# The late groups of a feed-forward network on seven products of halves: 256 tokens and a quarter of d_ff at a step, in place of 384 tokens and an eighth

## The chip, the cores and the metric

The kernel runs on one core of a Trainium2 chip. The metric is the device time of one execution in microseconds. The engines are named as in the profile: PE is TensorE (products), PEld its weight loads, DVE VectorE, ACT ScalarE, POOL GpSimd, SP the engine that issues most of the transfers.

## What is computed

Eight batches of eight heads, 576 tokens, head size 64, with 32 memory slots per head; then a feed-forward network on 4608 tokens (512 to 2048 to 512).

```python
a = exp(phi - max_over_tokens(phi)); a = a / (sum(a) + 1e-09)      # phi: 8,8,576,32
k_m = einsum('bhsm,bhsd->bhmd', a, k)
v_m = einsum('bhsm,bhsd->bhmd', a, v)
scores = q @ k_m^T / sqrt(64)
attn = softmax(scores)                                             # over 32 slots
x = (attn @ v_m)  as 4608 x 512
h = x @ w_in                                                       # 512 x 2048
out = maximum(0.01 * h, h) @ w_out                                 # 2048 x 512, all in float32
```

## The kernel before

v_m and w_in are multiplied first, batch by batch: the folded matrix W (256 rows of heads and slots by 2048) takes the place of v_m and w_in, so that a token needs attn @ W. That is the fold: `fold(b, j)` makes quarter j of W of batch b, with 24 small products on parts of the array (L722). A product of two float32 matrices is three products of 16-bit halves: high by high, low by high, high by low. A high half is made by ScalarE (a CAST or a scaled copy), the low one by DVE (value less high half). Of W, ScalarE makes the high half (L745) and DVE the low one (L746).

The feed-forward network runs over 12 groups G of 384 tokens (three for two batches) and 8 units u of 256 columns of d_ff each. `up_products` (L806) multiplies the tokens' attention weights a by W into a bank of PSUM, two banks a unit (f16: 6 products of 384 columns for each half of a unit, or 12 of 192 in the groups that lie across two batches). `activate` applies the leaky rectifier with ScalarE (Prelu, L813), makes the high half g with DVE (L821) and the low half (L822). `down` (L861) multiplies g by w_out into three banks, 18 products of 512 columns a unit, and keeps on adding to them over all units of the group; `store` (L840) scales and sends 128 rows.

All five engines run in the order in which the code issues: there is no scheduler. `OPENING` is a list of steps written by hand: group G0, in float32, with the loading of the weights, batches 0 and 1, and products of ones (`z`, L928) that fill gaps. Then comes `slot(n)` for each unit n from 5 on: ups of unit n+3, fold, attention steps of the list `before`, `activate`, the splits of the fold, attention steps of `after`, down of unit n, attention steps of `ends`. The lists say at which slot which step of the attention of a later batch runs: A1 to C4 make the softmax of phi, C10 the product with k and v (L485), D and Q transposes (L600 for Q), E10 to E22 the scores (L621), S01 the maximum over memory slots (L655, DVE), S02 its subtraction (L658, GpSimd), S03 the exponential (L663, ScalarE), S04 to S08 the normalisation and the halves of a (L685, L689, L693). The table `SPLIT` spreads the making of the halves of w_in and w_out (`k`: L279 ScalarE, `l`: L284 DVE) over slots 6 to 22.

## Time and profile before

| what | value |
|---|---|
| median of 3 runs | 689.25 us (688.81 to 689.81) |
| profiled execution | 688.93 us, of it 687.2 us span |
| granted TensorE clock, mean | 0.992 |
| busy: PE, PEld | 673.7 us, 371.1 us |
| busy: DVE, ACT, POOL | 390.9 us, 269.8 us, 52.9 us |
| instructions | 14105 |

The span goes from the first to the last instruction; what the runs' time has above it lies around it. Busy times are shares of the span per engine. Matmuls of one stream overlap in the records, so the distance between two starts, and not the duration of one, says what a product costs in a stream.

### The profile page before, as it was taken

The page shows a single profiled execution, that of the slowest core. Times are in us where ns is not written, and L with a number is a line of the kernel's source. Part 1 is how long each engine was busy: PE and PEld are TensorE (multiplying, and loading weights), DVE is VectorE, ACT ScalarE, POOL GpSimd, SP SyncE. Part 2 cuts the span into 40 slices and gives each one's busy share as a digit, 9 for nine tenths or more (in the row PEclk, how much of TensorE's full clock was granted, in tenths as well). Part 3 has the DMA queues.
Part 4 walks back from the last instruction along what each step waited for, and adds up shares of the span by engine and source line. Part 5 has one row for each costly group of instructions (what it writes and reads, how often), then busy time and mean ns, then how long its engine had stood idle before and what let it go on. Part 6 is the DMA issues. An engine that isn't in the chain of part 4 may idle for free.

```text
span 687.2 us, 14105 instructions
## 1 busy us (share of the span) xinstructions
PE 673.7 (98%) x6142; PEld 371.1 (54%) x6142; DVE 390.9 (57%) x586; ACT 269.8 (39%) x441; POOL 52.9 (8%) x42
## 2 busy tenths in 40 slices
PE   7899999999999999999999999999999999999997
PEld 6545446665454546665545445565545545655553
DVE  5775876966887563445685473544584654332220
ACT  2699666643444323312332432421332342322321
POOL 0000130000210120000120120000120030000000
PEclk9799999999999999999999999999999999999999
DMA  9999504613503400204503500303500100100101
GB/s 267 401 317 281 201 1 143 179 47 109 135 16 125 115 1 1 82 2 138 150 1 124 128 5 1 82 1 105 139 12 2 48 1 1 47 2 0 47 1 46
DMA packets 32590, 60.16 MB, mean 88 GB/s; under 512 B 4368, under 2 KB 14608, under 8 KB 32528
## 3 DMA queue, kind: packets, MB, share of 16 engines
q1 hardware_dynamic: 32240, 58.87, 28.5%
q8 instruction: 48, 0.79, 0.5%
q10 hardware_dynamic: 288, 0.39, 0.2%
q14 instruction: 14, 0.11, 0.1%
HBM read 49.81 MB, written 9.44 MB: 86 GB/s over the span
## 4 chain that ended last, share of the span: by engine, by line
PE 94%; DVE 2%; issue 1%; ACT 1%; DMA 1%; ACTq 0%; DVEq 0%
PE po L861 55%; PE ph L806 29%; PE pa L722 4%; PE pa L621 2%; PE pa L485 2%; DMA out_dram<-ob 1%; PE pa L550 1%; PE pa L436 0%; DMA wi<-in_phi_dram 0%; DVE W L746 0%; DVE r1k L406 0%; PE pa L211 0%; ACT wi L274 0%; PE pa L499 0%; ACT ob L840 0%
## 5 line engine op out<-in xcount | busy, mean ns | idle before, releaser
L861 PE MATMUL po<-wo,g 128*128 128x512 f16 (+1 forms) x1680 | 399.5, 392 | 0.0
L861 PEld LDWEIGHTS <-g 128*128 128x128 f16 x1584 | 152.7, 98 | 183.1 <-issue 11.0
L806 PE MATMUL ph<-a,W 128*128 128x192 f16 (+2 forms) x1504 | 210.9, 293 | 0.1
L813 ACT ACTIVATE gf<-ph,g_sc 128x384 f32<-128x384 f32 x176 | 99.4, 580 | 220.0 <-PE ph L806 175.3
L821 DVE CAST g<-gf 128x768 f16<-128x768 f32 x88 | 61.6, 700 | 190.7 <-ACT gf L813 190.6
L806 PEld LDWEIGHTS <-W 128*128 128x128 f16 x1440 | 129.2, 98 | 55.0 <-issue 5.1
L822 DVE TENSOR_TENSOR g<-gf,g 128x768 f16<-128x768 f32 x88 | 84.3, 958 | 3.0
L658 POOL TENSOR_TENSOR t<-t,tm 128x1152 f32<-128x1152 f32 (+2 forms) x9 | 15.9, 1770 | 429.7 <-DVE tm L655 429.7
L722 PE MATMUL pa<-wi,vT 64*32 64x512 f16 (+1 forms) x704 | 29.9, 420 | 2.4 <-issue 2.0
L746 DVE SCALAR_TENSOR_TENSOR W<-pa,W 128x512 f16<-128x512 f32 x48 | 30.7, 681 | 0.0
L861 PEld LDWEIGHTS po<-wo,g 128*128 128x128 f32 x96 | 17.6, 190 | 21.0 <-issue 19.4
L840 ACT ACTIVATE ob<-po,osc 128x512 f32<-128x512 f32 x28 | 18.8, 688 | 25.1 <-PE po L861 23.2
L745 ACT ACTIVATE W<-pa 128x512 f16<-128x512 f32 x48 | 26.1, 599 | 2.4 <-PE pa L722 1.9
L600 DVE STREAM_TRANSPOSE ld<-ld 96x1536 f32<-96x1536 f32 x14 | 24.0, 1750 | 2.2 <-PE pa L485 2.2
L663 ACT ACTIVATE t<-t 128x1152 f32<-128x1152 f32 (+2 forms) x10 | 9.7, 972 | 33.8 <-POOL t L658 31.4
L260 ACT ACTIVATE ld<-ld 128x768 f32<-128x768 f32 (+1 forms) x24 | 19.9, 840 | 4.3 <-DMA ld<-in_moe_w_in_dram 4.2
L693 POOL TENSOR_TENSOR a<-t,a 128x1152 f16<-128x1152 f32 (+2 forms) x9 | 18.5, 2053 | 40.0 <-ACT a L689 35.8
L635 DVE STREAM_TRANSPOSE t<-pa 128x384 f32<-128x384 f32 x24 | 12.3, 557 | 15.1 <-PE pa L621 15.1
L520 ACT ACTIVATE x_k<-pa,r 128x192 f32<-128x192 f32 x14 | 5.1, 417 | 39.7 <-PE ph L806 38.1
L689 ACT CAST a<-t 128x1152 f16<-128x1152 f32 (+2 forms) x9 | 8.7, 970 | 26.9 <-DVE t L685 26.9
L806 PEld LDWEIGHTS ph<-a,W 128*128 128x128 f32 x64 | 12.1, 199 | 9.6 <-issue 3.5
L485 PE MATMUL pa<-ld 64*32 64x128 f32 x1008 | 16.1, 271 | 0.5 <-issue 0.5
(157 smaller groups left out, 428.6 us busy)
## 6 DMA issues: line engine op xcount, KB each, us to landing
ld<-in_q_dram SPq DMA_DIRECT2D x16, 576.0 KB, 6.6
out_dram<-ob SPq DMA_DIRECT2D x138, 64.0 KB, 1.7
ld<-in_k_dram SPq DMA_DIRECT2D x28, 288.0 KB, 5.0
ld<-in_v_dram SPq DMA_DIRECT2D x28, 288.0 KB, 5.6
ld<-in_moe_w_in_dram SPq DMA_DIRECT2D x12, 512.0 KB, 7.3
ld<-in_moe_w_out_dram SPq DMA_DIRECT2D x12, 512.0 KB, 7.6
ld<-in_phi_dram SPq DMA_DIRECT2D x7, 576.0 KB, 7.5
ld<-in_moe_w_in_dram SPq DMA_DIRECT2D x8, 256.0 KB, 8.2
```

The costliest lines, as they stand in the source:

```text
L260: nc.scalar.activation(hi.bitcast(F32), hi.bitcast(F32), AF.Prelu, scale=2.0**-111, alpha=-(2.0**32))
L485: nc.tensor.matmul(var["pk"][g][hh * M:(hh + 1) * M, cs], ld["phi"][rows, hh, j, :], ld["kv", hh][rows, kinds[0]:kinds[-1] + 1, j, :], sta ...
L600: nc.vector.transpose(flat, ld["q", g].rearrange("p hh j d -> p (hh j d)"))
L722: nc.tensor.matmul(pf[g][cols, :], lhs, rhs, start=(n == 0), stop=(n == len(passes) - 1), tile_position=(g * D, hh * M),)
L745: nc.scalar.activation(w[:, g, 0], src[g], AF.Copy, scale=ws)
L746: nc.vector.scalar_tensor_tensor(w[:, g, 1], src[g], ws, w[:, g, 0], ALU.mult, ALU.subtract)
L806: nc.tensor.matmul(ph[:, t0:t0 + n * SB], lhs, rhs, start=(m == 0), stop=(m == len(seq) - 1))
L813: nc.scalar.activation(dst, ph, AF.Prelu, scale=sc, alpha=SLOPE)
L821: nc.vector.tensor_copy(g[:, 0], gf)
L822: nc.vector.tensor_tensor(g[:, 1], gf, g[:, 0], ALU.subtract)
L840: nc.scalar.activation(ob, po, AF.Copy, scale=so)
L861: nc.tensor.matmul(po, lhs, rhs, start=(f == 0 and m == 0), stop=(f == NQ * NF - 1 and m == len(seq) - 1),)
```

## The change

G0 to G2 (the first two batches) stay as they were. From token 1152 on there are 13 groups of 256 tokens and one of 128, with four steps each: a step k takes a quarter of d_ff (512 columns, two units). A group's output is a 2x2 matter: two halves of tokens by two halves of the 512 output columns, summed over two halves of the d_ff of the step. The eight products of such halves are replaced by seven with sums and differences of the operands (Winograd's form). For this:

- The sums of blocks of w_out are made once, in slots 5 to 15: GpSimd adds (`add_up`, L347), ScalarE makes the high half (`hi_sum`, L350), DVE the low one (`lo_sum`, L353), 16 of 128x512 of each.
- The sums of g are made in each step: `add_g` four on DVE (L1052), `hi_g` two CASTs on ScalarE (L1056), `lo_g` two differences on DVE (L1060).
- `up_late` (L1017) makes four blocks a step, each 6 products of 256 columns (or two by six, where the group lies across two batches), in turn in the two halves of one bank; the Prelu (L1029) frees a half.
- `down_late` (L1084) takes 42 products of 256 columns a step, in four parts of 12, 12, 6 and 12, into four banks: `p1` and three of the group. After a group's fourth step `combine` adds them up (L1094 to L1103) and scales (L1106).
- The order of a step: up(0), part(0), up(1), part(1), `ends`, up(2), part(2), up(3), fold of step k+3 (L817, splits L841 and L842), part(3), `ends`. The ups are those of step k+2.
- Attention steps are placed by a table, batch to first slot and spread. The loads of Q move from the end of the batch before to behind C10 (here L562); S07 and S08 (L779, L784) write a in another layout, in three pieces; L735 is S01, L743 is S03, L680 the transposes of Q, L670 the low half of the averaged v, and L701 E1.
- `SPLIT` now carries the sums too, and keeps to slots 5 to 20. The products of ones become 9 of 512 columns in place of 40 of 128. h of two pieces of w_in moves from DVE to ScalarE.
- Buffers are cut by hand from one block of memory in place of pools. Scale factors change by powers of two.

```diff
-IDLE = (2, 3, 5, 7, 14)
+IDLE = (1, 3, 4)
-ENDS = {1: "A2", 2: "B0", 4: "C10 C2", 6: "D10 D11 D2", 7: "E1"}
+ENDS = {1: "A2", 2: "B0", 4: "C10 C2 q0 q1 phi+", 6: "D10 D11 D2", 7: "E1 kv0+ kv1+ kv2+ kv3+"}
+
+ATTENTION = {2: (8, 2), 3: (18, 3), 4: (35, 3), 5: (51, 3), 6: (75, 3), 7: (91, 3)}
...
+    def up_late(k, i):
...
+        ph = banks["ph"][:, i % 2 * EH:(i % 2 + 1) * EH]
+        fs = slice(i * P, (i + 1) * P)
+        for b, c0, n, t0 in parts(G):
+            w, a = states[b]["W"][j], a_columns(b)
+            seq = [
+                (w[:, g, x, fs], a[:, y, g, c0:c0 + n])
+                for g in range(NG) for x, y in ((0, 0), (1, 0), (0, 1))
+            ]
+            for m, (lhs, rhs) in enumerate(seq):
+                nc.tensor.matmul(
+                    ph[:, t0:t0 + n], lhs, rhs, start=(m == 0), stop=(m == len(seq) - 1)
+                )
...
+        nc.scalar.activation(dst, ph, AF.Prelu, scale=g_sc2[:, j:j + 1], alpha=SLOPE)
...
+    def add_g(k):
+        if not whole(G2 + k // NQ):
+            return
+        gf = late[k]["gf"].rearrange("p (s x) -> p s x", s=4)
+        gt = operands(k)[1]
+        for x, y, z, op in (
+            (0, gf[:, 0], gf[:, 2], ALU.add), (3, gf[:, 1], gf[:, 0], ALU.subtract),
+            (1, gf[:, 1], gt[:, 0], ALU.subtract), (2, gf[:, 3], gt[:, 1], ALU.add),
+        ):
+            nc.vector.tensor_tensor(gt[:, x], y, z, op)
+
+    def hi_g(k, h):
+        src, dst = operands(k)[h], operands(k)[2 + h]
+        nc.scalar.copy(dst[:, 0], src)
+
+    def lo_g(k, h):
+        src, dst = operands(k)[h], operands(k)[2 + h]
+        nc.vector.tensor_tensor(dst[:, 1], src, dst[:, 0], ALU.subtract)
...
+    PRODUCTS = (
+        (0, (0, 0), "p1", 0), (2, (1, 0), 0, 0), (4, 1, 0, 1), (6, 3, 1, 0), (3, 0, 1, 1),
+        (5, (1, 1), 2, 0), (1, 2, 2, 1),
+    )
...
+            for u in range(2):
+                for m, (x, y) in enumerate(((0, 0), (0, 1), (1, 0))):
+                    if isinstance(t, tuple):
+                        c0 = (2 * u + t[0]) * E + t[1] * EH
+                        rhs = wo_s[j][:, y, c0:c0 + EH]
+                    else:
+                        rhs = sums[j][:, t, y, u]
+
+                    nc.tensor.matmul(
+                        acc, g[:, x, s, u], rhs, start=(h == 0 and j == 0 and u == 0 and m == 0),
+                        stop=(j == NQ - 1 and u == 1 and m == 2), skip_group_check=True,
+                    )
...
+    def combine(G, n):
+
+        o = obs[:, 0:2 * E].rearrange("p (s e) -> p s e", s=4)
+        pair = [t.rearrange("p (s e) -> p s e", s=2) for t in pos[G]]
+        if n == 0:
+            nc.scalar.copy(o[:, 3], banks["p1"][:, 0:EH])
+            p1 = o[:, 3:4].broadcast_to([P, 2, EH])
+            nc.vector.tensor_tensor(o[:, 0:2], pair[0], p1, ALU.add)
+        elif n == 1:
+            nc.vector.tensor_tensor(o[:, 2], pair[1][:, 0], o[:, 1], ALU.add)
+        elif n == 2:
+            p5 = pair[1][:, 1].unsqueeze(1).broadcast_to([P, 2, EH])
+            nc.vector.tensor_tensor(o[:, 1:4:2], o[:, 1:3], p5, ALU.add)
+        else:
+            nc.vector.tensor_tensor(o[:, 1:3], pair[2], o[:, 1:3], ALU.add)
+            for t in (1, 0):
+                ob = obs[:, (1 - t) * E:(2 - t) * E]
+                nc.scalar.activation(ob, ob, AF.Copy, scale=row_scale(G, t))
+                send(G, t, ob)
...
+    def step(k):
+
+        n, c, m = NU * G2 + 2 * k, k + 1, k + 2
+        G, last = G2 + k // NQ, k % NQ == NQ - 1
+
+        def up(i):
+            if m < nq:
+                up_late(m, i)
+
+        def part(i):
+            if whole(G):
+                down_late(k, ((0, 1), (2, 3), (4,), (5, 6))[i])
+                if last and i > 0:
+                    for x in ((0, 1), (2,), (3,))[i - 1]:
+                        combine(G, x)
+            else:
+                down_tile(k, i)
+
+        up(0)
+        if c < nq:
+            lo_g(c, 0)
+            hi_g(c, 1)
+        run(before.get(n, ()))
+        part(0)
+        up(1)
+        if c < nq:
+            lo_g(c, 1)
+        run(after.get(n, ()))
+        part(1)
+        run(ends.get(n, ()))
+        up(2)
+        run(before.get(n + 1, ()))
+        part(2)
+        up(3)
+        rest = [(b, j, fold(b, j)) for b, j in folds_late(k + 3)]
+        if m < nq:
+            hi_g(m, 0)
+            add_g(m)
+        split_all(rest)
+        run(after.get(n + 1, ()))
+        part(3)
+        run(ends.get(n + 1, ()))
```

What this does to the order is shown at two places. The first is a fold in the middle of the late groups. On ACT, before: a unit's two Prelu (L813) and then the high halves of W (L745).

```order
L813 ACTIVATE gf<-ph,g_sc 128x384 [waits PE_49,Activation_49]
L813 ACTIVATE gf<-ph,g_sc 128x384 [waits PE_49]
L745 ACTIVATE W<-pa 128x512 [waits PE_49] x2
L813 ACTIVATE gf<-ph,g_sc 128x384 [waits DVE_49,PE_49,Activation_49]
L813 ACTIVATE gf<-ph,g_sc 128x384 [waits PE_49]
```

On DVE, before, at another fold of the same kind: the low halves of W (L746) stand behind the two halves of g, and the scale of the batch's output (L761, L765) follows.

```order
L821 CAST g<-gf 128x768 [waits Activation_49]
L822 TENSOR_TENSOR g<-gf,g 128x768 [waits DVE_49]
L746 SCALAR_TENSOR_TENSOR W<-pa,W 128x512 [waits Activation_49] x2
L761 TENSOR_SCALAR osc<-pv,pp_max 128x1
L765 COPY osc_t<-osc 64x1 [waits DVE_49]
```

On ACT after, w_mem is W, wi_87 the rectified g, arena the halves of g and of its sums, in the fold of the step:

```order
L1029 ACTIVATE wi_87<-ph,g_sc_99 128x2x128 [waits PE_49] x3
L1056 CAST arena<-wi_87 128x768 [waits Activation_49]
L841 ACTIVATE w_mem<-pa 128x512 [waits PE_49] x2
L1029 ACTIVATE wi_87<-ph,g_sc_99 128x2x128 [waits DVE_49,PE_49]
L1056 CAST arena<-arena 128x1024 [waits DVE_49]
```

On DVE after, at the same kind of place, a step in which a batch's first quarter is folded:

```order
L765 STREAM_TRANSPOSE t_4013<-t_3847 128x1152 [waits Pool_49]
L1052 TENSOR_TENSOR arena<-wi_87 128x256 [waits DVE_49,Activation_49]
L1052 TENSOR_TENSOR arena<-wi_87 128x256
L1052 TENSOR_TENSOR arena<-wi_87,arena 128x256 [waits DVE_49] x2
L842 SCALAR_TENSOR_TENSOR w_mem<-pa,w_mem 128x512 [waits Activation_49] x2
L857 TENSOR_SCALAR osc<-pv,pp_max 128x1
L862 COPY osc_t<-osc 64x1 [waits DVE_49]
L483 TENSOR_REDUCE r1k<-arena 128x128 [waits DMAHW4_49]
L1060 TENSOR_TENSOR arena<-wi_87,arena 128x768
L1060 TENSOR_TENSOR arena<-arena 128x1024 [waits Activation_49]
```

The high halves of W now stand behind the fourth Prelu of the step and the first CAST of g; the low halves stand behind the four sums of g, which want that Prelu, and ahead of the low parts of the next g.

The second place is the softmax of a batch. On DVE before, the maximum (L655) stands between two units' halves of g:

```order
L821 CAST g<-gf 128x768 [waits Activation_49]
L822 TENSOR_TENSOR g<-gf,g 128x768 [waits DVE_49]
L655 TENSOR_REDUCE tm<-t_3655 128x36
L406 TENSOR_REDUCE r1k<-ld 128x128 [waits DMAHW0_49]
L821 CAST g<-gf 128x768 [waits Activation_49]
L822 TENSOR_TENSOR g<-gf,g 128x768 [waits DVE_49]
L667 TENSOR_REDUCE ts__3716<-t_3655 128x36 [waits Pool_49]
```

On DVE after, the same maximum (L735) in a step that ends a group:

```order
L1096 TENSOR_TENSOR obs<-po,obs 128x512 [waits DMAHW4_49,DMAHW5_49,PE_49,Activation_49]
L1098 TENSOR_TENSOR obs<-po,obs 128x256 [waits DMAHW1_49,DMAHW6_49,DMAHW0_49,DMAHW7_49,DVE_49,PE_49]
L715 STREAM_TRANSPOSE t_3847<-pa 128x384 x3
L1101 TENSOR_TENSOR obs<-obs,po 128x2x256 [waits DVE_49,PE_49]
L1052 TENSOR_TENSOR arena<-wi_87 128x256 [waits Activation_49]
L1052 TENSOR_TENSOR arena<-wi_87 128x256
L1052 TENSOR_TENSOR arena<-wi_87,arena 128x256 [waits DVE_49] x2
L735 TENSOR_REDUCE tm<-t_3847 128x36
L1103 TENSOR_TENSOR obs<-po,obs 128x512 [waits PE_49]
L1060 TENSOR_TENSOR arena<-wi_87,arena 128x768 [waits Activation_49]
L1060 TENSOR_TENSOR arena<-arena 128x1024 [waits DVE_49,Activation_49]
L747 TENSOR_REDUCE ts__3929<-t_3847 128x36 [waits Activation_49]
```

On ACT before, the exponential (L663) stands behind three stores and a unit's two Prelu:

```order
L745 ACTIVATE W<-pa 128x512 [waits PE_49] x2
L840 ACTIVATE ob<-po,osc 128x512 [waits DMAHW3_49,DMAHW2_49,DMAHW4_49,DMAHW1_49,PE_49]
L840 ACTIVATE ob<-po,osc 128x512 [waits DMAHW6_49,DMAHW5_49,DMAHW7_49,DMAHW0_49,PE_49]
L840 ACTIVATE ob<-po,osc 128x512 [waits DMAHW3_49,DMAHW2_49,DMAHW4_49,DMAHW1_49,PE_49]
L813 ACTIVATE gf<-ph,g_sc 128x384 [waits PE_49,Activation_49]
L813 ACTIVATE gf<-ph,g_sc 128x384 [waits PE_49]
L663 ACTIVATE t_4293<-t_4293 128x1152 [waits Pool_49]
L813 ACTIVATE gf<-ph,g_sc 128x384 [waits PE_49,Activation_49]
L813 ACTIVATE gf<-ph,g_sc 128x384 [waits PE_49]
L745 ACTIVATE W<-pa 128x512 [waits PE_49] x2
```

On ACT after, the exponential is L743:

```order
L1029 ACTIVATE wi_87<-ph,g_sc_99 128x2x128 [waits PE_49] x2
L1056 CAST arena<-wi_87 128x768 [waits Activation_49]
L1106 ACTIVATE obs<-obs,osc 128x512 [waits DMAHW4_49,DMAHW3_49,DMAHW5_49,DMAHW2_49,DVE_49]
L1106 ACTIVATE obs<-obs,osc_t 128x512
L1029 ACTIVATE wi_87<-ph,g_sc_99 128x2x128 [waits PE_49]
L1056 CAST arena<-arena 128x1024
L743 ACTIVATE t_3847<-t_3847 128x1152 [waits Pool_49]
L1029 ACTIVATE wi_87<-ph,g_sc_99 128x2x128 [waits PE_49] x3
L1056 CAST arena<-wi_87 128x768 [waits Activation_49]
L1029 ACTIVATE wi_87<-ph,g_sc_99 128x2x128 [waits DVE_49,PE_49]
```

On DVE the maximum now stands between the sums of g and the last addition of the combination (L1103). On ACT the two scalings (L1106) wait for that addition and stand ahead of the next step's first Prelu, and the exponential, which waits for GpSimd, ahead of its other three.

384 lines of the change are left out of this document (262 added, 122 removed).

## The prediction

> **What bounds the kernel now.** I read the page first, its shares, its slices and its chain, and then single groups.
>
> ```profile
> span 687.2 us, 14105 instructions
> PE 673.7 (98%) x6142; PEld 371.1 (54%) x6142; DVE 390.9 (57%) x586; ACT 269.8 (39%) x441; POOL 52.9 (8%) x42
> ...
> PE   7899999999999999999999999999999999999997
> ...
> DVE  5775876966887563445685473544584654332220
> ACT  2699666643444323312332432421332342322321
> ...
> PEclk9799999999999999999999999999999999999999
> ...
> PE 94%; DVE 2%; issue 1%; ACT 1%; DMA 1%; ACTq 0%; DVEq 0%
> PE po L861 55%; PE ph L806 29%; PE pa L722 4%; PE pa L621 2%; PE pa L485 2%; DMA out_dram<-ob 1%; PE pa L550 1%; PE pa L436 0%; DMA wi<-in_phi_dram 0%; DVE W L746 0%; DVE r1k L406 0%; PE pa L211 0%; ACT wi L274 0%; PE pa L499 0%; ACT ob L840 0%
> ```
>
> TensorE is busy in 98% of the span and is 94% of the chain that ended last; its clock was full except at the start. L861 (down) and L806 (up) alone are 84% of the chain. DVE is at 57%, but at 4 to 9 tenths until slice 32: an engine with room on the average, not everywhere. So the kernel is a stream of products, and a change pays by what it takes from the stream, and costs by every gap that it opens in it. The busy times of the matmul groups overlap, so I price by distance between starts:
>
> ```profile
> 403.45 2.11 PE L806 MATMUL ph<-a,W 128*128 128x384 f16 x12
> 405.49 0.84 PE L722 MATMUL pa<-wi,vT 64*32 64x512 f16 x24
> 406.27 4.06 PE L861 MATMUL po<-wo,g 128*128 128x512 f16 x18
> ...
> 410.16 2.11 PE L806 MATMUL ph<-a,W 128*128 128x384 f16 x12
> 263.93 2.14 PE L806 MATMUL ph<-a,W 128*128 128x192 f16 x24
> 265.91 4.05 PE L861 MATMUL po<-wo,g 128*128 128x512 f16 x18
> ```
>
> Eighteen 128x512 fill 406.27 to 410.16: 216 ns each. Twenty-four 128x192 fill 263.93 to 265.91: 82.5 ns. Twelve 128x384 and the change to the fold's small tiles (0.09 us, an estimate from the same switch in other rows, which costs nothing here) end after 2.04 us: 162.5 ns. A line through 192 and 384 columns gives 109.2 ns for 256, 55.8 for 128 and 29 for 64; it gives 216 for 512 as well, as measured. The fold L722 holds TensorE 0.78 us, with its switches 0.86.
>
> **What the products cost, before and after.** G0 to G2 stay. For batches 2 to 7, 9 groups by 8 units, before: 576 ups of 384 columns, 576 of 192, 1296 downs of 512: 93.6+47.5+279.9 = 421.0 us. After, 13 whole groups of 256 tokens and one of 128: ups 864 of 256 columns, 288 of 192, 288 of 64 and 288 of 128 (groups that cross from batch to batch, and the last one); downs 52 steps by 42 = 2184 of 256 columns and 48 of 512: 94.3+23.8+8.4+16.1 and 238.5+10.4 = 391.5 us. Saving 29.5 us. Two prices are not in the trace: 64 and 128 columns. Their ends are the line (29 and 55.8) and the nearest row, 82.5 at 192 columns, which would take back 15.4 and 7.7 us. I take the line, since no floor shows down to 192.
>
> ```profile
> L861 PEld LDWEIGHTS <-g 128*128 128x128 f16 x1584 | 152.7, 98 | 183.1 <-issue 11.0
> ```
>
> The 98 ns of a weight load are longer than 82.5, so loads overlap already at 192 columns, but 64 must hide more of them. [...]
>
> **What the other engines get.** In each late step DVE does four sums (L1052), two differences (L1060); ScalarE four Prelu (L1029) and two CASTs (L1056); every fourth step the four banks are combined (L1094 to L1106). The nearest rows:
>
> ```profile
> L837 ACT ACTIVATE ob<-po,osc 128x256 f32<-128x256 f32 x1 | 0.5, 474 | 1.9 <-DMA out_dram<-ob 1.9
> L468 DVE TENSOR_TENSOR wi<-wi 128x256 f32<-128x256 f32 x1 | 0.4, 424 | 0.0
> L689 ACT CAST a<-t 128x768 f16<-128x768 f32 x1 | 0.8, 832 | 1.4 <-DVE t L685 1.4
> L689 ACT CAST a<-t 128x1152 f16<-128x1152 f32 (+2 forms) x9 | 8.7, 970 | 26.9 <-DVE t L685 26.9
> L745 ACT ACTIVATE W<-pa 128x512 f16<-128x512 f32 x48 | 26.1, 599 | 2.4 <-PE pa L722 1.9
> L746 DVE SCALAR_TENSOR_TENSOR W<-pa,W 128x512 f16<-128x512 f32 x48 | 30.7, 681 | 0.0
> L822 DVE TENSOR_TENSOR g<-gf,g 128x768 f16<-128x768 f32 x88 | 84.3, 958 | 3.0
> L655 DVE TENSOR_REDUCE tm<-t 128x36 f32<-128x1152 f32 x6 | 8.1, 1345 | 0.0
> L658 POOL TENSOR_TENSOR t<-t,tm 128x1152 f32<-128x1152 f32 (+2 forms) x9 | 15.9, 1770 | 429.7 <-DVE tm L655 429.7
> L663 ACT ACTIVATE t<-t 128x1152 f32<-128x1152 f32 (+2 forms) x10 | 9.7, 972 | 33.8 <-POOL t L658 31.4
> L840 ACT ACTIVATE ob<-po,osc 128x512 f32<-128x512 f32 x28 | 18.8, 688 | 25.1 <-PE po L861 23.2
> L445 DVE TENSOR_TENSOR wi<-wi,pa 128x512 f32<-128x512 f32 x1 | 0.7, 679 | 0.0
> L600 DVE STREAM_TRANSPOSE ld<-ld 96x1536 f32<-96x1536 f32 x14 | 24.0, 1750 | 2.2 <-PE pa L485 2.2
> ```
>
> A step's stream is 24x109.2 + 42x109.2 = 7.2 us; ScalarE's share is 4x0.474+0.83+1.03 = 3.8, DVE's 4x0.42+0.96+1.28 = 3.9 (1024 columns by the line between the nearest rows). Neither becomes the bound on average; it is order that counts.
>
> **Wait 1, the fold.** Before, fold, 18 downs (3.89 us) and up follow each other, and the folded W is read a whole group later: the low split (L746) ended here 4.7 us after the fold without a gap on TensorE.
>
> ```profile
> 406.74 1.08 ACT L745 ACTIVATE W<-pa 128x512 f16<-128x512 f32 x2
> 406.87 1.92 DVE L821 CAST g<-gf 128x768 f16<-128x768 f32 x1 [2.17 <-ACT gf L813]
> ...
> 409.70 1.28 DVE L746 SCALAR_TENSOR_TENSOR W<-pa,W 128x512 f16<-128x512 f32 x2
> L821 DVE CAST g<-gf 128x768 f16<-128x768 f32 x88 | 61.6, 700 | 190.7 <-ACT gf L813 190.6
> ```
>
> (L745 is ScalarE's part, the high half, two in 1.08 us; L746 DVE's, two in 1.28. Queued instructions thus follow each other 0.05 to 0.1 us faster than their means add up, and I count the chains below so.) After, the W folded in a step behind up(3) is read by up(0) of the next step, with only part(3), twelve products, 1.31 us, in between. Count from the last issue of up(3). TensorE wants the first low half of W at 0.86+1.31+0.11 = 2.28 us, for the second product of up(0). ScalarE: the product lands about 0.2 later, Prelu ends at 0.68, CAST (768 columns) at 1.55, the two L841 at 2.1 and 2.6. DVE: four L1052 from 0.71 to 2.28, 0.39 each, then two L842 to 2.92 and 3.58. TensorE waits 0.69 for the first low half, issues three products, and waits 0.33 for the second: 1.02 us, and 0.85 where small attention products stand in between; I take 0.92 for each of twenty steps, 18.4. What is queued behind L842 on DVE (L1060, the low parts of g) is wanted only a part later and is covered. In the first fold of four batches three CASTs of the softmax (L779) stand ahead of the Prelu, 0.36 more each, 1.4. In three steps C10 (L562) stands behind part(3); its bank is freed only by L842, and it waits 0.45 longer than up(0) would, 1.4. The first late step costs 1.5, with two groups of operands made at once. Sum 22.7 us.
>
> **Wait 2, the softmax.** For batches 4 to 7 the maximum (L735) now stands on DVE behind L1052 and ahead of the last combination, L1103, in a step that combines. DVE: L1052 to 2.28, L735 to 3.6, L1103 to 4.25. ScalarE: two L1106 to 5.55, Prelu(0) of the next step to 6.0, CAST (1024) to 7.0, then the exponential L743, ready since GpSimd's 3.6+2.13 = 5.73, to 8.1, and Prelu(1) to 8.5. The four ups share the two halves of one bank, so up(2) waits for Prelu(0): due at 5.25, it goes at 6.05; up(3) waits for Prelu(1): due at 7.36, it goes at 8.5. That is 1.9 us, four times, 7.6. For batch 3 the maximum comes ahead of part(1) in the combining step, so that L1098 and both L1106 are late as well: I take two and a half times as much, 4.7. Sum 12.3 us. Before, the same softmax steps opened no such gap: the two ups of a unit had a bank each, and g was made two slots ahead of its downs.
>
> **Wait 3, E1 and small ones.** E1 (L701) reads what L670 writes behind two transposes of Q (3.5 us) on DVE; half a step of products (3.3 to 3.9 us) covers most: 0.5 for four batches, 2.2 for batch 3 with L1060 in between: 4.2 us. The first combination frees its bank late at 13 places by 0.05, and the step ahead of the last groups waits 0.65: 1.3 us.
>
> **The early sums.** In slots 5 to 15, 16 sums on GpSimd, 16 L350 on ScalarE and 16 L353 on DVE are new.
>
> ```profile
> L658 POOL TENSOR_TENSOR t<-t,tm 128x384 f32<-128x384 f32 x2 | 1.7, 834 | 67.6 <-DVE tm L655 67.6
> L658 POOL TENSOR_TENSOR t<-t,tm 128x768 f32<-128x768 f32 x1 | 1.5, 1486 | 0.6 <-DVE tm L655 0.6
> L279 ACT ACTIVATE wo<-wo,sw 128x512 f16<-128x512 f32 x4 | 2.9, 720 | 0.0
> L284 DVE SCALAR_TENSOR_TENSOR wo<-wo,sw,wo 128x512 f16<-128x512 f32 x4 | 3.0, 745 | 0.1
> 103.00:115.00 12.00, 12.00 (x84) 7.07 (x83) 5.83 (x9) 6.53 (x12) 0.00 (x0) 1.00 0.27 67
> 115.00:130.00 15.00, 14.91 (x138) 9.36 (x136) 14.30 (x20) 9.87 (x18) 0.00 (x0) 1.00 1.03 295
> 130.00:152.00 22.00, 22.00 (x298) 14.06 (x283) 16.59 (x22) 10.21 (x16) 0.00 (x0) 1.00 0.06 18
> ...
> ld<-in_q_dram SPq DMA_DIRECT2D x16, 576.0 KB, 6.6
> ```
>
> In the rows of the stretches, columns are the stretch, its length, then busy time (instructions) of TensorE, weight loads, DVE, ScalarE and GpSimd; the last row is the load of Q, with the time to landing at its end. DVE gets 11.9 us more, ScalarE 11.5, GpSimd 16.8 (1.05 each between its two rows). From 115 to 130 us DVE is busy 14.30 of 15, and the halves of w_out come through it; 103 to 115 has 6.2 us free, 130 to 152 has 5.4. If all is spread, nothing; if all 11.9 queue ahead of a down, what exceeds 5.4: up to about 6.5. I take 1. The opening's idle products go from 40 of 128 columns to 9 of 512, and two parts of w_in move from DVE to ScalarE: nothing, with ends of -1.5 and +1.5, since TensorE waits there for other engines. The loads of a batch's Q are issued behind C10 of that batch, three half steps (10.8 us) ahead of the transposes that read them; they landed after 6.6 us, so they are covered, as are phi, K and V, issued a batch ahead.
>
> **The sum.** The profiled run took 688.93 us, span 687.2 and 1.73 around it; the median of the runs is 689.25, 0.32 above, and I go by it: 689.25 - 29.5 + 22.7 + 12.3 + 4.2 + 1.3 + 1.0 = 701.25. The waits, 41.5 us, outweigh the saving by 12.
>
> **Rivals.** (1) The waits are shorter, and the kernel is faster. Wait 1's chain holds seven queued instructions (Prelu, four L1052, two L842), Wait 2's twelve, Wait 3's some five. If each goes x sooner than I count, 20x7 + 6x12 + 5x5 = 237 times x comes back; from x = 0.05 us the change is even, and at 0.1 it is 23.7 better: 677.5. For it: 0.05 is an eighth of a 256-column sum, and its price hangs on one row of one instruction. Against it: the row says 424, the pairs at 406.74 and 409.70 are already counted with their overlap, and L821 takes 2.04 and 1.92 against a mean of 700 ns when GpSimd works beside it, which would make x negative. (2) Products of 64 and 128 columns cost what 192 do: +23.1, 724; half of it 713. For it: the weight load of 98 ns; against it: the line that holds down to 192. (3) DVE is the bound in slots 8 to 16: +5.5, 707. For it: the 14.30 of 15. (4) A product of 256 columns costs more than the line says, because its load doesn't hide: the ends are the rows at 192 and 384 columns, 82.5 and 162.5 ns; 9.7 ns above the line eats the whole saving (29.5 over 3048 products), 731. Against it: 192 columns lie on the same line as 512. [...]
>
> **Numbers.** Slower by the gaps as counted, 690.7 to 710: 0.57. Rival 1: 0.19 faster, and 0.05 for coming out even. Rival 2: 0.09; rival 3: 0.09; rival 4: 0.01, all slower. A change of 0.2%, 1.4 us, is about what a measurement can tell. Faster 0.19, same 0.05, slower 0.76. The range, 677 to 713, leaves out rival 1's better half and the upper part of rivals 2 and 4, under 2 in 10; the forecast's own range is 691 to 710.
>
> **What would show it.** L1017, the ups of the late steps, should have gaps on TensorE released by DVE L842 of 0.6 to 1.0 us at twenty places; by ScalarE L1029 ahead of up(2) and up(3) at five; the busy share of TensorE should fall from 98% to about 93%, with the downs at 109 ns. The prediction is wrong if L1017 shows no gaps released by L842, if the 64-column products stand 80 ns apart, or if slots 8 to 16 open a gap of more than 5 us.

## The result and the profile after

The changed kernel took 740.1 us (median; 736.9 to 744.5), the kernel before 689.0 beside it: a ratio of 1.074 [1.071, 1.077]. The forecast had the side right and the size wrong: 51 us slower, not 12, and outside the range of 677 to 713. The profiled run took 739.38 us.

The page of the kernel after, in the lines shown of before:

```profile
span 737.4 us, 17620 instructions
PE 669.9 (91%) x7592; PEld 487.3 (66%) x7592; DVE 526.4 (71%) x829; ACT 398.9 (54%) x677; POOL 82.6 (11%) x71
...
PE   7799998989999988999889988999988998899996
...
DVE  5857859988975657867877786666787868664641
ACT  3888755736445445554555455554455635555543
...
PEclk9999999999999989999999999999999999999999
...
PE 38%; DVE 14%; ACT 8%; issue 2%; DMA 1%; POOL 0%; DVEq 0%; ACTq 0%; POOLq 0%
PE po L1084 17%; PE ph L1017 14%; DVE arena L1052 7%; DVE w_mem L842 3%; PE ph L1084 3%; ACT wi L1029 3%; ACT obs L1106 2%; PE pa L562 1%; PE po L1116 1%; PE pa L701 1%; DVE obs L1103 1%; DMA arena<-in_v_dram 1%; ACT arena L1056 1%; ACT a L779 1%; DVE obs L1096 1%
```

DVE rose from 57% to 71%, ScalarE from 39% to 54%, and neither is the bound by its share. Yet the chain that was 94% TensorE now runs through DVE and ScalarE for 22% of the span, and TensorE's slices, 9 before from the third to the last but one, change between 8 and 9 to the end: it loses a little everywhere. The waits of TensorE's instructions, first in the early part (from the first down in f16, that of unit 8, to the first late step), then from there to the end (us in total, times, longest); in the kernel before the same view of 114 to 687 us has no row:

```profile
PE ph L903 <- ACT arena L910: 5.3, 2, 2.6
PE ph L1017 <- ACT wi L1029: 2.8, 5, 0.6
PE ph L903 <- DVE w_mem L842: 2.3, 3, 1.6
...
PE ph L1017 <- ACT wi L1029: 19.9, 16, 2.5
PE ph L1017 <- DVE w_mem L842: 14.2, 28, 1.8
PE po L1084 <- DVE obs L1098: 2.4, 2, 2.0
```

The view leaves out short waits. Taken by distance between starts, less the price of the product in between, the whole difference of the spans comes out (us; gaps are excesses of over 0.1 us):

| part | before | after | difference |
|---|---|---|---|
| opening, to the first down in f16 | 114.1 | 112.2 | -1.9 |
| full-size products, at their prices at full clock | 516.3 | 486.8 | -29.5 |
| small tiles (folds, attention) | 46.4 | 51.6 | +5.2 |
| gaps ahead of the first late step | 0.9 | 14.8 | +13.9 |
| gaps in the late steps | 0.0 | 52.9 | +52.9 |
| shorter excesses, some 8 us of them at half clock | 4.9 | 14.6 | +9.7 |

That is +50.3 (the spans differ by 50.2). The row of the full-size products is count by price, with the forecast's own prices; that the prices hold is shown further below. Of the 5.2 us of the small tiles, 1.7 are a half-clock stretch in E1 of batch 3, the rest short stops inside C10 (2.3) and E1 (1.3). The late gaps are 22.7 us behind Prelu (L1029), about as much behind the fold (L842 20.9, L841 1.1, C10 0.6), 4.6 behind L1098, and 3 of smaller kinds.

One group end in a softmax step, in the timeline of the kernel after (start, duration, engine, instruction, in brackets the idle time and its releaser):

```profile
352.92 1.35 DVE L735 TENSOR_REDUCE tm<-t 128x36 f32<-128x1152 f32 x1
353.36 0.82 PE L1084 MATMUL po<-wo,arena 128*128 128x256 f16 x6
...
354.19 0.68 DVE L1103 TENSOR_TENSOR obs<-po,obs 128x512 f32<-128x512 f32 x1
...
354.90 0.72 ACT L1106 ACTIVATE obs<-obs,osc 128x512 f32<-128x512 f32 x1 [2.62 <-DVE obs L1103]
355.53 0.71 ACT L1106 ACTIVATE obs<-obs,osc_t 128x512 f32<-128x512 f32 x1
...
356.14 0.45 ACT L1029 ACTIVATE wi<-ph,g_sc 128x256 f32<-128x256 f32 x1
...
356.65 0.82 PE L1017 MATMUL ph<-a,w_mem 128*128 128x256 f16 x6 [2.47 <-ACT wi L1029]
```

The six downs ahead of the wait start at 353.36 and need 0.65 us, 109 ns each. The next up can't go: it shares its bank with the up before it, whose Prelu stands on ScalarE behind two scalings (L1106), which wait for the last sum of the group (L1103), which stands on DVE behind the maximum. One wait of 2.5 us.

The first fold of a batch:

```profile
368.61 2.84 POOL L784 TENSOR_TENSOR a<-t,a 128x384 f16<-128x384 f32 x3 [5.66 <-ACT a L779]
...
369.77 1.97 DVE L1052 TENSOR_TENSOR arena<-wi 128x256 f32<-128x256 f32 x2 [1.78 <-ACT wi L1029]
...
371.65 0.87 DVE L1052 TENSOR_TENSOR arena<-wi,arena 128x256 f32<-128x256 f32 x2
372.44 1.28 DVE L842 SCALAR_TENSOR_TENSOR w_mem<-pa,w_mem 128x512 f16<-128x512 f32 x2
373.18 0.24 PEld L1017 LDWEIGHTS <-w_mem 128*128 128x128 f16 x3 [1.94 <-DVE w_mem L842]
```

The first two sums of 256 columns take 1.97 us beside GpSimd, the last two 0.87 without it.

### The profile page after: what moved, and what is told of

Same layout as the page of the kernel before. It is cut to its first block, busy times and chain, and to the rows that moved or that the text cites. A ratio compares the mean times of both kernels' runs of the same rounds, so it can differ in the third digit from the quotient of the medians.

```text
span 737.4 us, 17620 instructions
## 1 busy us (share of the span) xinstructions
PE 669.9 (91%) x7592; PEld 487.3 (66%) x7592; DVE 526.4 (71%) x829; ACT 398.9 (54%) x677; POOL 82.6 (11%) x71
## 3 DMA queue, kind: packets, MB, share of 16 engines
q1 hardware_dynamic: 32432, 59.13, 26.7%
## 4 chain that ended last, share of the span: by engine, by line
PE 38%; DVE 14%; ACT 8%; issue 2%; DMA 1%; POOL 0%; DVEq 0%; ACTq 0%; POOLq 0%
PE po L1084 17%; PE ph L1017 14%; DVE arena L1052 7%; DVE w_mem L842 3%; PE ph L1084 3%; ACT wi L1029 3%; ACT obs L1106 2%; PE pa L562 1%; PE po L1116 1%; PE pa L701 1%; DVE obs L1103 1%; DMA arena<-in_v_dram 1%; ACT arena L1056 1%; ACT a L779 1%; DVE obs L1096 1%
## 5 line engine op out<-in xcount | busy, mean ns | idle before, releaser
L1084 PEld LDWEIGHTS <-arena 128*128 128x128 f16 x2184 | 211.9, 99 | 38.3 <-issue 13.4
L1017 PE MATMUL ph<-a,w_mem 128*128 128x256 f16 (+3 forms) x1728 | 188.0, 248 | 39.2 <-ACT wi L1029 22.7
L1029 ACT ACTIVATE wi<-ph,g_sc 128x256 f32<-128x256 f32 (+1 forms) x224 | 104.1, 465 | 215.2 <-PE ph L1017 215.1
L1017 PEld LDWEIGHTS <-w_mem 128*128 128x128 f16 x1728 | 137.8, 98 | 70.5 <-issue 30.6
L1084 PE MATMUL po<-wo,arena 128*128 128x256 f16 x936 | 125.5, 275 | 3.1 <-DVE obs L1098 2.4
L1084 PE MATMUL po<-arena 128*128 128x256 f16 x936 | 122.6, 274 | 0.0
L970 PE MATMUL po<-wo,arena 128*128 128x512 f16 (+1 forms) x384 | 108.3, 434 | 0.0
L1052 DVE TENSOR_TENSOR arena<-wi 128x256 f32<-128x256 f32 x104 | 47.6, 499 | 79.9 <-ACT wi L1029 79.5
L1060 DVE TENSOR_TENSOR arena<-arena 128x1024 f16<-128x1024 f32 x52 | 64.3, 1237 | 33.0 <-ACT arena L1056 33.0
L1060 DVE TENSOR_TENSOR arena<-wi,arena 128x768 f16<-128x768 f32 (+1 forms) x60 | 60.8, 1015 | 10.7 <-ACT arena L1056 10.6
L903 PE MATMUL ph<-a,w_mem 128*128 128x192 f16 (+2 forms) x304 | 54.6, 329 | 8.1 <-ACT arena L910 4.1
L1056 ACT CAST arena<-arena 128x1024 f16<-128x1024 f32 x52 | 53.8, 1035 | 2.2 <-DVE arena L1052 2.2
L970 PEld LDWEIGHTS <-arena 128*128 128x128 f16 x288 | 27.8, 98 | 33.5 <-issue 2.5
L1056 ACT CAST arena<-wi 128x768 f16<-128x768 f32 (+1 forms) x60 | 46.3, 774 | 1.7
L1052 DVE TENSOR_TENSOR arena<-wi,arena 128x256 f32<-128x256 f32 x104 | 43.8, 421 | 1.8
L1084 PE MATMUL ph<-wo,arena 128*128 128x256 f16 x312 | 43.2, 275 | 0.0
L903 PEld LDWEIGHTS <-w_mem 128*128 128x128 f16 x240 | 21.6, 101 | 14.3 <-issue 5.5
L842 DVE SCALAR_TENSOR_TENSOR w_mem<-pa,w_mem 128x512 f16<-128x512 f32 x48 | 30.8, 682 | 0.1
L817 PE MATMUL pa<-wi,vT 64*32 64x512 f16 (+1 forms) x704 | 28.9, 420 | 0.4 <-ACT vT L650 0.4
L784 POOL TENSOR_TENSOR a<-t,a 128x384 f16<-128x384 f32 x22 | 23.0, 1070 | 48.1 <-ACT a L779 43.6
```

The costliest lines, as they stand in the source:

```text
L784: nc.gpsimd.tensor_tensor(lo[:, tb], t2[:, tb], hi[:, tb], ALU.subtract)
L817: nc.tensor.matmul(pf[g][cols, :], lhs, rhs, start=(n == 0), stop=(n == len(passes) - 1), tile_position=(g * D, hh * M),)
L842: nc.vector.scalar_tensor_tensor(w[:, g, 1], src[g], ws, w[:, g, 0], ALU.mult, ALU.subtract)
L903: nc.tensor.matmul(ph[:, t0:t0 + n * SB], lhs, rhs, start=(m == 0), stop=(m == len(seq) - 1))
L970: nc.tensor.matmul(po, lhs, rhs, start=(f == 0 and m == 0), stop=(f == NQ * NF - 1 and m == len(seq) - 1),)
L1017: nc.tensor.matmul(ph[:, t0:t0 + n], lhs, rhs, start=(m == 0), stop=(m == len(seq) - 1))
```

## The experiments

Each version was timed beside the kernel before (medians 689.0 to 690.7). The runs of one version lie 2 to 8 us apart, so a difference of some 3 us between two versions is not clear of their scatter. TensorE's waits are those of the late part, by the view shown.

**x1_split_first.** The two splits of a folded W ahead of the sums of the step:

```
+        split_all(rest)
         if m < nq:
             hi_g(m, 0)
             add_g(m)
-        split_all(rest)
```

> The splits of the fold (L841 on ScalarE, L842 on DVE) are issued ahead of the CAST and the four sums of g. Theory 'queue': the 22 us of TensorE's waits on L842 come from the four L1052 and the CAST ahead of it; then the first low half is ready at 2.35 in place of 2.92 and the second at 2.95, waits go from about 1.0 to 0.35 a fold, in the first folds of four batches (L1052 slowed by GpSimd) from 2.4 to 0.6: about 14 us less, 726. Rival 'copy': the high halves on ScalarE or the fold itself are late, whatever stands ahead on DVE: 738 to 742.

736.7 us: 3.5 less than the kernel after, which the scatter does not separate from nothing, though a wait of 14 us was taken away.

```profile
PE ph L1017 <- ACT wi L1029: 27.0, 15, 2.5
PE po L1084 <- DVE obs L1098: 5.3, 7, 2.0
...
PE ph L1017 <- DVE w_mem L842: 0.6, 2, 0.3
```

L842 is all but gone from the view (14.2 to 0.6), and Prelu and L1098 took over (19.9 to 27.0, 2.4 to 5.3): at the five group ends that also fold, the wait behind Prelu went from about 0.85 to 2.3. The queue that delayed the fold was real, but what now stands behind it ends later.

**x3_scale_later.** The two scalings (L1106) of a group go behind the second Prelu of the next step (`scale_out()` after `up(1)`) instead of ahead of its first.

> The two scalings of a finished group (L1106) are issued behind the second Prelu of the next step instead of ahead of its first. Theory 'order on ScalarE': of the 22.7 us that TensorE waits for a Prelu (L1029) all at group ends without softmax goes (0.85 four times, 1.4 three times), and at the five with softmax the wait moves to up(2), behind the exponential, 2.2 in place of 3: 10 to 12 us less, 729. Rival: the combination on DVE (L1103) and the exponential set these waits and the scalings only stand beside them: 3 us less at most, 737.

729.6 us, 10.5 less, as the theory of L1106 had it:

```profile
PE ph L1017 <- DVE w_mem L842: 14.3, 29, 1.8
PE ph L1017 <- ACT wi L1029: 8.9, 6, 2.0
```

**x5_two_banks.** Every second up in a bank of its own:

```
-        ph = banks["ph"][:, i % 2 * EH:(i % 2 + 1) * EH]
+        ph = banks["p1" if i % 2 else "ph"][:, EH:]
```

> The odd ups write into the second half of p1's bank, the even ones into the bank that all four share now, so that an up waits for the last Prelu but one. (Their start clears part of what p1 has summed, so the numbers of p1 are not kept.) Theory 'one bank': up(1) waits for Prelu(0) although it writes the other half, because both lie in one bank; with two, the group ends without softmax lose their waits (0.85 four times, 1.4 three times), those with softmax go from 3.0 to about 1.9, and the 0.07 at some 45 other places goes: 12 to 15 us less, 727. Rival: ScalarE is late by more than a part anyway, the wait moves to up(2): 3 us less at most, 737.

730.4 us, 9.7 less, short of the 12 to 15 expected: the waits behind Prelu fell from 19.9 to 7.8, but those for L841, the high half of W, rose from 0.5 to 5.4. (What an odd up clears of p1's sums is left out of the result here and in y4.) That the two halves of one bank make an up wait for the Prelu just before it is thus shown: by this run, and by ups that follow each other in slots 21 to 23 of the kernel after, each six products long (0.65 us) and 1.38 us from the next:

```profile
225.44 0.82 PE L1017 MATMUL ph<-a,w_mem 128*128 128x256 f16 x6 [0.56 <-ACT wi L1029]
226.82 0.82 PE L1017 MATMUL ph<-a,w_mem 128*128 128x256 f16 x6 [0.56 <-ACT wi L1029]
```

**y1_split_scale.** x1 and x3 together, the scalings one each behind the second and the third Prelu.

> Both edits at once: the splits of the fold ahead of the sums of g, and the two scalings L1106 behind the second and the third Prelu of the next step. Theory 'one chain': the splits alone brought 3.5 us in place of 14, because the sums of g, now later, make L1103 and with it L1106 and the next Prelu late at the four group ends with a fold (2.3 us in place of 0.85); with the scalings out of the way that cost goes, and the two edits bring more than their sum: 25 us less than the changed kernel, 715. Rival 'sum': the two add up, 3.5 and 10.5: 726.

711.8 us: 28 less, twice the sum of the two alone (3.5+10.5).

```profile
PE ph L1017 <- ACT wi L1029: 8.0, 4, 2.0
PE po L1084 <- DVE obs L1098: 5.3, 7, 2.0
```

L842 is down to 1.2. The two waits lay one behind the other on the same queues, so that either edit alone let the other's remain. One thing is not held apart: y1 has its second scaling one Prelu later than x3.

**y2_softmax.** y1, and the maximum half a step earlier, the exponential behind the second Prelu, L1098 behind part(2) in place of part(1).

> As the run before, and besides: the maximum S01 and the subtraction S02 of a batch half a step earlier, ahead of the sums of g, the exponential S03 behind the second Prelu, and the second addition of the combination (L1098) behind part(2) with the third. Theory: the waits at the softmax steps (2.3 to 2.6 us, five of them, and 2.2 for L1098 of batch 3) go down to about 0.5 each, and the 0.26 for L1098 at each group end, which is a wait of part(2) for a read of its bank, goes: 14 us less than the run before, 701. Rival: DVE is so full at these steps that the wait turns up at the next operand: 4 us less, 711.

703.1 us, ratio 1.020 [1.017, 1.022]: 37 less than the kernel after, by order alone. L1098 is gone from the waits, and 9.2 us behind Prelu (14 places, 1.2 at most) remain.

**y4_banks and y5_cast_act.** On y2: the banks of x5; or the CAST of g in units 8 to 15 on ScalarE.

> As the run before, with the odd ups in the second half of p1's bank (the numbers of p1 are not kept). Theory 'one bank': what is left of waits for a Prelu, 0.07 us in some 45 places and the remains at group ends, goes: 5 to 7 us less than the run before, 695. Rival: nothing is left for it to win once ScalarE's order is mended: 1 us less at most.

> As y2_softmax, with the high halves of g of units 8 to 15 (L921) made by ScalarE in place of DVE. Theory 'DVE is full in slots 8 to 16': DVE gets 5 us of room there, and the first late step starts 3 to 6 us earlier: 697. Rival 'queues': the waits come from ScalarE standing behind the sums (L350 waiting for GpSimd), and more work for it makes them longer: 701 to 704.

701.4 and 703.5 us: 1.6 less, within the scatter, and no gain. The second bank took the waits behind Prelu from 9.2 to 3.1 us, but 4.6 of waits for L841 came in their place. Taking work from DVE moved it to a ScalarE queue that TensorE waits for as well: ahead of the first late step the waits for L842 went from 2.3 to 0.2 us, those for Prelu (L910) from 5.3 to 6.1.

**x4_no_sums, z1_adds_only, z2_no_adds: the early sums.** x4 makes none of the operands of sums of w_out; z1 keeps GpSimd's sums (L347) and leaves their halves (L350, L353) out; z2 keeps the halves and leaves the sums out. GpSimd clears what isn't written (x4 in slots 17 to 20, z1 in 20 to 23, z2 in slot 5).

> The 16 sums of blocks of w_out (GpSimd L347, ScalarE L350, DVE L353) are left out, their places in memory are cleared in slots 17 to 20; all products run as before. Theory 'early sums': the waits of 3.0, 3.1 and 2.8 us in slots 8 to 16 are theirs, and the first late step starts 8 to 10 us earlier: 731. Rival: these waits come from the steps of the attention, which now stand elsewhere, and stay: 738 to 741.

> The changed kernel with GpSimd's 16 sums of w_out kept and their halves (L350 on ScalarE, L353 on DVE) left out; the places of the halves are cleared in slots 20 to 23. Theory 'GpSimd beside DVE': what costs in slots 8 to 16 is that DVE's instructions take up to twice as long while GpSimd adds; unit 14's downs then start at 165 us or later (158.6 without any sums, 168.2 with all). Rival 'work': the 23 us of halves cost it; unit 14 starts at 160 or sooner. By the whole time 733 or less, and the clearing in slots 20 to 23 may cost some 5 of it again.

> The other part alone: GpSimd's sums of w_out are left out, ScalarE and DVE make the halves of what stands in the buffers (cleared once in slot 5). Theory 'GpSimd beside DVE': unit 14 starts at 161 us or sooner, since nothing waits for GpSimd and nothing is slowed by it. Rival 'work': 165 or later. The whole time 733 by the theory, 738 by the rival.

Whole times 743.8, 746.6, 731.7. The clearing disturbed the first two: in x4 a CAST that takes 0.65 us in the mean of the kernel after took 6.84 beside two clearings, and TensorE waited 4.25.

```profile
187.80 6.96 POOL L1201 MEMSET arena<- 128x4096 f16 x2
188.33 6.84 DVE L921 CAST arena<-arena 128x768 f16<-128x768 f32 x1
```

So they are read by when the down of unit 14, ahead of any clearing but z2's, starts. The rows are of the kernel after, x4, z1 and z2, in this order:

```profile
168.24 4.06 PE L970 MATMUL po<-wo,arena 128*128 128x512 f16 x18
```

```profile
158.61 4.05 PE L970 MATMUL po<-wo,arena 128*128 128x512 f16 x18
```

```profile
165.37 4.05 PE L970 MATMUL po<-wo,arena 128*128 128x512 f16 x18
```

```profile
159.72 4.05 PE L970 MATMUL po<-wo,arena 128*128 128x512 f16 x18
```

The kernel before starts it at 158.74. All sums and halves cost 9.6 us, GpSimd's sums alone 6.8, the halves alone 1.1. (The first downs in f16 start up to 0.8 us apart. Ahead of unit 14 the kernel after has two half-clock stretches, at 130.71 and 164.84; in the second the twelve ups just ahead of that down take 3.61 us, in x4, z1 and z2 1.95, so that such a stretch can hold 1.7 of these microseconds.) How GpSimd costs TensorE is seen in the kernel after:

```profile
118.41 0.72 ACT L350 ACTIVATE arena<-arena,sw 128x512 f16<-128x512 f32 x1 [0.82 <-POOL arena L347]
119.04 2.36 ACT L322 ACTIVATE wo<-wo,sw 128x768 f16<-128x768 f32 x3
...
119.93 1.71 POOL L347 TENSOR_TENSOR arena<-wo 128x512 f32<-128x512 f32 x1 [1.56 <-DVE arena L353]
120.44 2.02 DVE L327 SCALAR_TENSOR_TENSOR wo<-wo,sw,wo 128x768 f16<-128x768 f32 x1
121.31 1.03 ACT L910 ACTIVATE arena<-ph,g_sc 128x384 f32<-128x384 f32 x2
...
121.92 1.31 PE L903 MATMUL ph<-a,w_mem 128*128 128x192 f16 x14 [2.64 <-ACT arena L910]
```

ScalarE's halves wait for GpSimd, the Prelu stands behind them in ScalarE's queue, and TensorE waits for the Prelu. Beside GpSimd's sums a split of w_out (L327) takes 2.02 us; its mean was 1.01 before (the same split, then L284) and is 1.38 after. As z1 loses 6.8 of the 9.6 without any halves, the slowed work of DVE seems to be the greater part, and ScalarE's wait for GpSimd the smaller.

**y6_spread, y7_dve_adds.** y6 spreads the high and low parts of g, the scalings and the exponential over the step in another way; y7 is y6 with the sums of w_out on DVE.

> As y2_softmax, but ScalarE's work is spread over a step: the CAST of the sums of g behind the second Prelu (it stood ahead of it and waited for L1052, which GpSimd's subtraction slows from 0.4 to 1 us each), its low half behind the third, the scalings behind the first and the third, the exponential behind the first. Theory 'order on ScalarE': the 11 us that TensorE still waits for a Prelu go down to 3 or less: 695. Rival: L1052, slowed beside GpSimd, sets these waits, and they turn up at the next operand of a down: 701.

> As the run before, with the 16 sums of w_out on DVE in place of GpSimd. Theory 'GpSimd beside DVE': DVE gets 11 us more to do but is no longer slowed, and no add waits behind a low half on another engine: the first late step starts 2 to 5 us earlier, 692. Rival 'work': DVE is full there, each added microsecond is one of TensorE: 3 to 8 us more, 700.

720.9 and 718.1 us. y6 was worse than y2: its first scaling went ahead of the second Prelu and there waited 4.88 us for the last sum of the group in the softmax steps. y7 against y6 is the test of GpSimd: the first late step came 5.2 us sooner (229.7 to 234.9), of which 2.3 stand ahead of the first down in f16, and the whole took 2.8 less, within the scatter.

**w1_no_gpsimd.** The kernel after, with all of GpSimd's arithmetic from batch 2 on, the sums too, on DVE.

> The changed kernel with all of GpSimd's arithmetic from batch 2 on and the sums of w_out (L738, L752, L784, L347) on DVE, nothing else moved. Theory 'GpSimd beside DVE': DVE's instructions on two operands run at half their speed while GpSimd works, so that DVE loses nearly as much as it would take to do the work itself; the first folds of four batches go from 2.4 to about 1 us, the sums cost 5 us less, the exponential is ready 0.8 us sooner: 728. Rival 'work': DVE gets some 36 us more at its busiest places: 745 or more.

748.9 us, 8.8 more. GpSimd slows DVE (two sums took 1.97 us beside it for 0.87), but to give DVE its work is dearer in the late steps: the waits for L842 fell from 14.2 to 8.3 us, those behind Prelu grew from 19.9 to 26.7, and 5.2 for L784, now on DVE, are new.

**y8_waits_gone, y9_spread_more, y10_defer.** Three more orders, built on y7 (the scalings in fixed later steps, lo(g) at another place, each up reading the low halves of W last, the softmax over two or three steps; y9 also places the first late ups anew, y10 the attention of batch 3).

> As y7_dve_adds, with what it got wrong at the softmax steps mended (the first scaling L1106 stood ahead of the second Prelu and waited 4.5 us for L1103): the scalings one and two steps later, exponential and normalisation behind the third Prelu, at those steps the CAST of the sums of g behind the fold; and each up reads the low halves of W last. Theory 'the products save what was counted and the waits are all of the loss': of the 31 us of waits left after slot 24 some 5 remain, TensorE's clock stays full, and the kernel comes out at 684 to 690, at or below the kernel before. Rival 'something else': seven products of halves cost more than the trace of single products shows, and the time stays above 697 though the waits are gone.

> As y8_waits_gone, with the softmax of a batch over three steps in place of two and begun one step sooner, so that GpSimd's normalisation (L752) no longer falls on the sums of g (it made two L1052 take 2.56 us, and TensorE wait 2.1 to 2.9 at five places), and the first eight late ups half ahead of and half behind the downs of their slot. Theory 'the waits are all of the loss': the five waits go, and with them four stretches of TensorE at half its clock (1.7 us each); 9 + 7 + 2 us less, 687 to 692, as fast as the kernel before. Rival: DVE stays full in these steps and the wait turns up later; 700 or more.

> As y8_waits_gone, with the CAST of the sums of g behind the fold in the step after the exponential too (there GpSimd's L752 slowed the sums, and the CAST held the second Prelu for 2.1 us), and batch 3's attention half a step sooner. Theory 'the waits are all of the loss': the five waits of 2.1 to 2.9 us go down to 1 us or less and the half-clock stretches behind them go: 9 + 5 us less, 690 to 695. Rival: the wait turns up at the following step in full; 702 or more.

707.2, 703.0, 705.6 us: none reached the 684 to 695 expected. In y9 the waits for Prelu and L842 were nearly gone, and others stood in their place:

```profile
PE pa L497 <- DVE r1k L483: 5.9, 2, 3.0
PE pa L562 <- DVE w_mem L842: 4.5, 3, 1.5
PE ph L1017 <- ACT wi L1029: 2.6, 4, 0.8
```

After three such misses order no longer looked like the whole of it. The next run asks whether the work itself is too much for queues in order.

**v1_no_g_sums.** y8 without the four sums of g (L1052) of each late step and without the halves of these sums: 2.9 us of DVE and 1.0 of ScalarE less in each of 52 steps; every product stays.

> As y8_waits_gone, with the sums of g (L1052) and their halves (the second L1056 and L1060 of each step) left out; their places are cleared once, and TensorE runs all of its products on what stands there. It frees DVE of 2.9 us and ScalarE of 1.0 us in each of 52 steps. Theory 'the products save what was counted and DVE's and ScalarE's work for them costs it': of the 22 us of waits after slot 24 some 6 stay, the half-clock stretches go, and the kernel takes 680 to 687, below the kernel before. Rival 'the products': 2184 products of 256 columns in place of 1296 of 512 don't save 29 us, and it stays at 697 or more.

681.7 us, ratio 0.988 [0.985, 0.991]. Its page, and all its waits from 228 us on:

```profile
span 680.8 us, 17264 instructions
...
PE 653.0 (96%) x7592; PEld 484.1 (71%) x7592; DVE 379.1 (56%) x588; ACT 350.0 (51%) x625; POOL 57.4 (8%) x55
...
PE pa L562 <- issue: 1.8, 2, 1.3
PE pa L576 <- issue: 1.7, 1, 1.7
```

With the same 7592 products the waits for DVE and ScalarE are gone, and the late gaps, by distance between starts, are some 7 us against 21 to 22 in y8, and the mean granted clock is 0.995, for 0.979 in y8. The operands that are not made are zeros here; the products' distances are the same as in y8 (109 ns at 256 columns). So the seven products do save what they were counted at, and what costs more than they save is the making of the sums of g. That no order could hide that work is not shown: none of those tried did. Of the versions that leave nothing out, y9 (703.0) and y2 (703.1) are the quickest, and the kernel before is 2% faster than either.

## Why the prediction was wrong

The forecast had 12 us of loss, the spans show 50. The 38 between them are, by the rows of the table, 12.4 of late gaps (52.9 for 40.5 in Waits 1 to 3), 12.9 of gaps ahead of the first late step (13.9 for the 1.0 of the early sums), 9.7 of shorter excesses, most of them the clock, and 5.2 of small tiles, neither of which was in the sum, less 1.9 in the opening. The step that failed by its mechanism is Wait 2; the early sums were mis-sized, and the clock was left out.

**The products held.** 256, 192, 128 and 64 columns follow each other after 109, 83, 56 and 29 ns (medians), where the line gave 109.2, 82.5, 55.8 and 29. In a row of the timeline products of two sizes stand together; this up is six of 64 columns and six of 192, and takes 0.67 us to the next start, 6x(29+82.5):

```profile
319.34 0.83 PE L1017 MATMUL ph<-a,w_mem 128*128 128x64 f16 x12
320.01 0.82 PE L1084 MATMUL po<-arena 128*128 128x256 f16 x6
```

Rivals 2 and 4 are out.

**Wait 1 held in place; that its sum fits is partly luck.** L842 is the releaser and the late waits are 22.6 us for a forecast 22.7. But an ordinary fold cost 0.7 to 1.2, mostly 0.8, for the 0.92 counted (whose first wait, 2.92 less 2.28, is 0.64 and not 0.69). C10 waited 0.7 for 1.4, and the first late step shows none of its 1.5. Against that the first folds of four batches cost 2.2 to 2.8 rather than 1.28, since GpSimd's L784 slows the first two of the four sums (1.97 us for the two at 369.77), which the working had at 0.39 each.

**Wait 2 failed: the step that says which Prelu an up waits for.** I had up(2) wait for Prelu(0) and up(3) for Prelu(1), as if the halves of a bank were two buffers. Each up waited for the Prelu just before it, as the ups in slots 21 to 23 show, 1.38 us apart for 0.65 of products. So the delay behind L1106 reaches TensorE as one wait, and at every group end, not only in the softmax steps: 22.7 us of late waits, at 16 places in the view, and 3.6 in slots 21 to 23, for a forecast 12.3. x3 and x5 took over half of it away, each by another link of the same chain. No run took the wait alone away, so whether the bank itself asks for it is not shown.

**The early sums failed in size.** I took 1.0 without working it out, and gave 6.5 as the bound; by the down of unit 14 they cost 9.6. The bound counted only DVE's added work; it left out that GpSimd slows DVE's own splits (2.02 us for 1.01), and that ScalarE's halves wait for GpSimd with Prelus queued behind them. The prediction named a gap of over 5 us in slots 8 to 16 as what would show it wrong, and in sum they are that (no single one is over 2.8). That is rival 3 in place, with another mechanism.

**The small ones.** L1098 was 0.05 at 13 places; it measured about 0.3 at eight places, 2.2 in batch 3 and 4.6 in all. E1 was dearer in the forecast, 4.2, than on the chip: 1.1 in gaps and 1.3 in short stops.

**The clock was not in the sum.** In the kernel after TensorE's granted clock halved for 3.41 us at a time, from 35 us on at 130.7, 164.8, 260.4, 274.1, 373.1 and 543.7 us, and in the kernel before at no place between 35 and 686. Stretches of the kernel after, each 3.41 us long (TensorE's busy time follows the length; the clock stands ahead of the last two columns):

```profile
352.57:355.98 3.41, 1.61 (x15) 1.29 (x14) 3.40 (x4) 1.08 (x2) 1.56 (x1) 1.00 0.18 63
355.98:359.40 3.42, 2.52 (x22) 2.11 (x22) 3.22 (x3) 2.98 (x5) 0.57 (x1) 1.00 0.49 119
540.31:543.72 3.41, 0.99 (x10) 0.74 (x8) 3.41 (x3) 1.70 (x4) 2.13 (x1) 1.00 0.08 27
543.72:547.14 3.42, 3.38 (x17) 2.32 (x17) 3.21 (x3) 2.35 (x3) 0.00 (x0) 0.50 0.58 144
```

Products of 256 columns are 213 ns apart in these stretches, for 109 outside: up to 1.7 us lost in each, 8 to 9 in all. Ahead of four of the six TensorE had waited 1.8 to 2.6 us in one piece, ahead of those at 130.7 and 260.4 in several of 0.2 to 1.6. But of ten waits of 1.8 us or more from 112 us on only these four were followed by half clock: the one of 2.64 us at 119.3 left the clock full, and so did that of 2.47 up to 356.65. y2, with no wait of over 1.2 us behind Prelu, had a mean granted clock of 0.993, for 0.984 in the kernel after. The last section shows what tells such waits apart.

**And the waits don't add.** The forecast priced each wait by itself and summed. x1 gave 3.5, x3 10.5, both 28. What one queue in order delays is late for the next, and the three misses of y8 to y10 repeated my error: each moved work out of one wait's way and into another's.

## What to carry to other kernels

A change that trades products for operands is priced by the step in which the operands are made: list each engine's queue there in order, with every instruction that TensorE waits for, and follow the chain through all of them, since a delay on one queue is handed on to the next (here DVE was 71% busy and ScalarE 54%, and TensorE waited all the same). Two halves of one bank were not two buffers here: with a second bank (x5) the waits behind Prelu went from 19.9 to 7.8 us, of which 4.9 came back behind L841. Work put on GpSimd was not free for DVE (a split of w_out took 2.02 us beside it for 1.01), and four of ten waits of 1.8 us or more on TensorE were followed by up to 1.7 more through its clock.

## What the runs showed of the hardware

The clock halved behind waits shorter than the 3.41 us that it then stayed so: ahead of four half-clock stretches of the kernel after TensorE had waited 1.80, 2.03, 2.46 and 2.64 us in one piece.

What tells these waits from those that left the clock full can be read from the same trace. The starts of the six stretches lie 34.1, 95.6, 13.7, 99.0 and 170.6 us apart, which is 10, 28, 4, 29 and 50 times 3.41 to 3.43: they stand on a grid of their own length. The wait of 2.46 us that ends at 543.76 lies in one grid stretch, with 0.99 of 3.41 us busy, and the next is at half clock. The wait of 2.47 that ends at 356.65 is cut by a grid line; its stretches are busy for 1.61 and 2.52, and the clock stays full. From 110 to 735 us five grid stretches have TensorE idle for 1.83 to 2.64 us, and each was followed by one at half clock. Of the others, idle for 1.80 at most, only one was, that ahead of 260.41, with 1.09 us idle between the small tiles of E1. This is a count in one trace: no run moved a wait against the grid on purpose.

GpSimd slowed DVE by more than I had taken: two sums of 256 columns took 1.97 us beside it for 0.87, a split of w_out 2.02 for 1.01, a CAST of one operand 6.84 for 0.65 beside two clearings of 6.96 together. The CAST seems to stand still rather than to run slowly: in the kernels before and after each of the 11 CASTs of g that took over 0.9 us ended 0.41 or 0.42 us behind the end of an instruction of GpSimd, and the one of x4 0.41. What held it is not shown.
